# A retention and mixture-of-experts kernel: the second-to-last expert's chain two stages a step, and weight places given out earlier

## The chip, the cores and the metric

The kernel runs on one core of a Trainium2 chip. The metric is device time in microseconds of one execution; a run's time is compared with that of other runs of the same kernel. Engines: PE (TensorE, matmuls), DVE (VectorE), ACT (ScalarE), POOL (GpSimd) and SP, which here only issues DMAs. Each engine works through its own list of instructions in order and waits on semaphores.

## The reference

Three parts follow each other, all in float32:

```python
for t in range(S):                       # retention, 4 x 8 heads, S = 768, D = 64
    state = gamma * state + outer(k[t], v[t])
    y[t] = scale * q[t] @ state
# x: 3072 rows x 512.  Top-1 mixture, E = 8 experts, F = 1024
e = argmax(x @ w_gate)
out[i] = gate[i] * sigmoid(x @ w_output_gate)[i, e] * (relu(x[i] @ w1[e]) @ w2[e])
# soft mixture, 32 slots = 8 experts x 4
logits = out @ phi
slot_input = softmax(logits, over rows).T @ out
slot_out = relu(slot_input @ m_w1[e]) @ m_w2[e]
result = softmax(logits, over slots) @ slot_out
```

## The kernel before

Some 327 us are not touched by the change (retention, the gates, the lists of rows of each expert, and the stages of the first seven experts); only the stages of the last expert, and what follows, are.

The top-1 mixture goes expert by expert (`e`, 0 to 7, in an order set at run time), and each expert in KF = 8 stages `f`; `g = 8e + f` counts them. Stage `g` is `l1(g)` (L916 to L929): 12 matmuls of 128x128 by the expert's rows (L924: four k-tiles, each as w1-high by x-high, w1-high by x-low, w1-low by x-high), into one of two PSUM tiles, and one `relu` on ACT that leaves `h`. What the stage needs: the row of w1 (`load_w`, L214, three tiles `r`, issued three stages ahead), and its splitting into high and low (`split_w`, ACT `wh` L222 and DVE `wl` L223, two stages ahead). A `load_w` can go out when the `split_w` of the row three earlier is through.

The output of an expert isn't formed row by row. Instead each expert has a chain that makes logits of its rows and adds its share to the 32 slots:

- `logits` (PE L954, in two halves, `lps`), from `h` and a product of w2 and phi; `logit_parts` (ACT `ls` L961, DVE `ll` L962); `logit_sum` (PE L975 twice, then DVE `msk` L977 and three small ones, L979 to L981).
- `p_exp` (ACT L985, L986), `p_tr` (DVE `pd` L991 and two small ones).
- `slot_h` (PE L1037, 96 small matmuls, from `hB`, the turned `h`, and `pd`), `slot_s` (four copies `gr`, two on DVE and two on ACT, L1044), `slot_t` (PE `gsum` L1050, DVE `gt` L1053), `slot_in` (PE `slo` L1059, with the eight `w` pieces of w2), `slot_acc` (DVE `acc` L1063).
- beside it `c_tr` (DVE L1000), `c_exp` (DVE and ACT, L1004 to L1007) and `c_put` (DVE L1013 to L1017, then scatters `ctok` from POOL, L1020); `mask` (POOL L967) is made for the next expert.

This chain runs one expert late: `behind(e - 1, f)` (L1068) is called in stage `f` of expert `e`, behind `l1(g)`, and gives the chain's next part:

```python
if f == 0: logits(e, 1); slot_in(e - 1) if e; h_tr(e, 6); h_tr(e, 7)
f == 1: logit_sum    f == 2: p_exp     f == 3: p_tr     f == 4: slot_h, c_tr
f == 5: slot_s, c_exp     f == 6: slot_t, c_put
if 2 < f < 7: load_w2(e, (2 * f - 6, 2 * f - 5))
```

(here `e` is the expert ahead). Its `slot_in` falls into stage 0 of the expert after the next, its `slot_acc` and the next `logit_parts` into stage 1 (L1118 to L1122). For expert 6 there is no such stage: its `slot_in` and `slot_acc` stand behind the loop (L1183, L1184), between `logit_parts` and `logit_sum` of expert 7. The chain of expert 7 runs there alone, from L1181 to L1217, and its result `siT` starts the last part.

The last part (from L1225) is the soft mixture on the 32 slots. `f_l1` (L1234) and `f_l2` (L1268) read the second mixture's weights, 128 pieces `m` of 128x512 (256 KB each), in the order in which they were loaded; `emit_out` writes the result, 12 outputs of 256 KB for each half of the columns. 92 of the pieces are loaded before `f_l1` starts, into whatever tiles are free by then (`load_m2`, L269): own tiles `m2p`, then tiles of the w1 rows (`wraw`, `whl`), of the rows x (`xtp`, `xp`), of w2 (`w2p`, eight tiles, `wup`), and of `h` (`hp`, `hbp`). The other 36 go into tiles freed by the last part (`refill`).

All those loads are issued by SP, in program order: `load_w`, `load_w2` (L945) and `load_m2`. A load whose tile is still read waits, and all behind it wait too.

For expert 7 the first four `w` pieces go into the tiles `xp` (the gathered rows, "row places", free from stage 0 on) in stage 2 (L1167), the last four into `whl` in stages 6 and 7 (L1171). The eight `w2p` tiles get pieces `m` behind the loop (L1192), the `xp` tiles at the very end (L1219).

Of the kernel before, what the change touches and what calls it, by code (L numbers as in the profile page):

```python
# [22 lines left out]
E = 8  # L23
# [114 lines left out]
def retention_moe_kernel(ctx, tc, qt, kt, kn, vn, gates, moe_w1, moe_w2,  # L138
# [57 lines left out]
    def load_er(k):  # L196
        if k < E:
            er.append(nc.values_load(ordi[0:1, k:k + 1], engines=[mybir.EngineType.SP], min_val=0, max_val=E - 1))
# [77 lines left out]
    def load_m2(pool, tag, w=1):  # L276
        w = min(w, NM2 - len(m2_t))
        if w > 0:
            m2_into(pool.tile([128, w * 512], F32, tag=tag, name="m2"), w, (pool, tag, w) if w < 3 else None)
# [601 lines left out]
    with ExitStack() as pb:  # L881
# [49 lines left out]
        def h_tr(e, f):  # L931

            c = C[e]
            if f == 0:
                hB[e] = hbp.tile([128, NBX, KF, 32], F32, tag="hB", name="hB")
            nc.vector.transpose(out=hB[e][:, 0:NB[e], f, :], in_=hs[e * KF + f][:, 0:c].rearrange("p (b t) -> p b t", t=32))  # L936
# [5 lines left out]
        def load_w2(e, fs, pool=w2p, tag="w2"):  # L942
            for f in fs:
                w2n[e, f] = pool.tile([128, DM], F32, tag=tag, name="w2")
                nc.sync.dma_start(out=w2n[e, f], in_=moe_w2[0, bass.ds(er[e], 1), :, f * DM:(f + 1) * DM].rearrange("o p d -> (o p) d"))  # L945

        def logits(e, hf):

            c = C[e]
            if hf == 0:  # L950
                lps[e] = ps_1.tile([128, c], F32, tag="l", name="lps")
            for i in range(4):
                f = hf * 4 + i
                nc.tensor.matmul(out=lps[e][32 * i:32 * i + 32, :], lhsT=wp[e][:, f, :], rhs=hs[e * KF + f][:, 0:c],  # L954
                                 start=(hf == 0), stop=(hf == 1), skip_group_check=True)

        def logit_parts(e):
            c = C[e]
            hi, lo = lrs[e] = [sp.tile([128, CX], F32R, tag=n, name=n) for n in ("ls", "ll")]
            ps = lps.pop(e)  # L960
            nc.scalar.activation(out=hi[:, 0:c], in_=ps, func=ACTF.Copy)  # L961
            nc.vector.tensor_tensor(out=lo[:, 0:c], in0=ps, in1=hi[:, 0:c], op=ALU.subtract)  # L962
# [7 lines left out]
        def logit_sum(e):  # L970

            c = C[e]
            ps = lrs2[e] = ps_1.tile([128, 512], F32, tag="r", name="lsum")
            for n, part in enumerate(lrs.pop(e)):
                nc.tensor.matmul(out=ps[:, 0:c], lhsT=same_r, rhs=part[:, 0:c], start=(n == 0), stop=(n == 1))  # L975
            lm = lms[e] = msks.pop(e)
            nc.vector.tensor_tensor(out=lm[:, 0:c], in0=ps[:, 0:c], in1=lm[:, 0:c], op=ALU.add)  # L977
            sm = sms[e] = sp.tile([128, 8], F32, tag="smb", name="smb", bufs=2)
            nc.vector.tensor_reduce(out=sm[:, 0:1], in_=lm[:, 0:c], axis=AX.X, op=ALU.max)  # L979
            nc.vector.tensor_tensor(out=sm[:, 1:2], in0=sm[:, 0:1], in1=mrun, op=ALU.max)  # L980
            nc.vector.tensor_scalar(out=sm[:, 2:3], in0=sm[:, 1:2], scalar1=-1.0, scalar2=None, op0=ALU.mult)  # L981

        def p_exp(e):
            c, sm, lm = C[e], sms[e], lms[e]
            nc.scalar.activation(out=lm[:, 0:c], in_=lm[:, 0:c], func=ACTF.Exp, bias=sm[:, 2:3], accum_out=sm[:, 3:4])  # L985
            nc.scalar.activation(out=sm[:, 4:5], in_=mrun, func=ACTF.Exp, bias=sm[:, 2:3])  # L986
# [54 lines left out]
        def slot_s(e):  # L1041
            grs[e] = sp.tile([128, 4, 256], F32, tag="gr", name="gr")
            for a in range(4):
                (nc.scalar.copy if a % 2 else nc.vector.tensor_copy)(out=grs[e][:, a, :], in_=gps[e][a])  # L1044
# [10 lines left out]
        def slot_in(e):  # L1055
            ps = slo[e] = ps_1.tile([128, DM], F32, tag="C", name="slo")
            for f in range(KF):
                i = f % 4
                nc.tensor.matmul(out=ps[32 * i:32 * i + 32, :], lhsT=gts[e][:, f, :], rhs=w2n.pop((e, f)),  # L1059
                                 start=(f < 4), stop=(f >= 4), skip_group_check=True)  # L1060

        def slot_acc(e):
            nc.vector.scalar_tensor_tensor(out=acc, in0=acc, scalar=sms.pop(e)[:, 4:5], in1=slo.pop(e), op0=ALU.mult, op1=ALU.add)  # L1063

        def behind(e, f):

            if not 0 <= e < E:
                return  # L1068
            if f == 0:
                logits(e, 1)  # L1070
                if e:
                    slot_in(e - 1)
                h_tr(e, 6)
                h_tr(e, 7)
            elif f == 1:
                logit_sum(e)
            elif f == 2:
                p_exp(e)
            elif f == 3:
                p_tr(e)  # L1080
            elif f == 4:
                slot_h(e)
                c_tr(e)
            elif f == 5:
                slot_s(e)
                c_exp(e)
            elif f == 6:
                slot_t(e)
                c_put(e)
            if 2 < f < 7:  # L1090
                load_w2(e, (2 * f - 6, 2 * f - 5))

        load_er(1)

        after(load_w(1), gets[0])
# [12 lines left out]
        for g in range(G):  # L1108
            e, f = divmod(g, KF)
            if f == 0:  # L1110
                load_er(e + 2)
            if e + 1 < E and f < len(XT[e + 1]):

                gather(e + 1, (f,))
                if f:
                    after(gets[e + 1][f], [relu[-1]])
            split_w(g + 2)
            if e and f == 1:  # L1118

                if e > 1:  # L1120
                    slot_acc(e - 2)
                logit_parts(e - 1)  # L1122
            if g < G - 3:
                load_w(g + 3)
            else:
                load_m2(wraw, "r1")
            if g > 3 and g % 2 and len(m2_t) < NPRE:
                load_m2(m2p, "m2", 2)
            if f in (4, 5) and e + 1 < E:
                for j in range(2 * f - 8, min(2 * f - 6, len(XT[e + 1]))):  # L1130
                    x_scale(e + 1, j)
            if f == KF - 1 and e + 1 < E:

                xps = x_mm(e + 1, "ABDr", sorted(((j, kk) for kk in range(KD) for j in range(len(XT[e + 1]))),
                                                 key=lambda b: XT[e + 1][b[0]] < 128))
                l1(g, lambda: [x_split(e + 1, ps) for ps in xps])
            else:
                l1(g)
            behind(e - 1, f)


            if g == UMM:
                wq_mm(0, ps_1, "C")
                wq_add(0)
            if f == (1 if e else UMM):
                wq_turn(e, sp.tile([128, KF, NS], F32, tag="wp", name="wp"))
            if e + 1 < E:
                if f == (2 if e else 3):
                    part_load(e + 1)
                if e == 0 and f in (3, 4):  # L1150
                    for q in ((1, 2), (3,))[f - 3]:
                        wq_load(1, q, 1, wup, "wu")
                if f == (3 if e else 6):

                    wq_mm(e + 1, ps_1, "A" if e else "C")
                    wq_add(e + 1)
            if g == KF - 1:
                wq_load(2, 1, 1, wup, "wu")
                wq_load(2, 2, 1, wup, "wu")
            if g == KF:  # L1160
                wq_load(2, 3, 1, wup, "wu")
            if e and e + 2 < E and 4 <= f < 7:
                wq_load(e + 2, f - 3, 1, wup, "wu")
            elif G - 13 < g < G - 9:
                load_m2(wup, "wu", 2)
            if g == G - 6:
                load_w2(e, range(4), xp, "xy")  # L1167
            if g >= G - 2:

                for i, tag in enumerate(("wh1", "wl1")):  # L1170
                    load_w2(e, (2 * f - 8 + i,), whl, tag)  # L1171
            if f == 4:
                logits(e, 0)
            if f == 5:

                mask(e)
            if f >= 5:
                h_tr(e, 2 * f - 10)
                h_tr(e, 2 * f - 9)
        e = E - 1  # L1180
        logits(e, 1)  # L1181
        logit_parts(e)
        slot_in(e - 1)  # L1183
        slot_acc(e - 1)  # L1184
        logit_sum(e)
        load_m2(whl, "wh1")
        load_m2(whl, "wl1")
        for _ in range(KD):
            load_m2(xtp, "xh")
            load_m2(xtp, "xl")  # L1190
        for _ in range(8):
            load_m2(w2p, "w2")  # L1192
        h_tr(e, 6)
        h_tr(e, 7)
        for _ in range(NH):
# [20 lines left out]
        c_exp(e)  # L1216
        c_put(e)  # L1217
        for _ in range(4):
            load_m2(xp, "xy")  # L1219
        for _ in range(2):  # L1220
            load_m2(whl, "wh1")
            load_m2(whl, "wl1")
# [162 lines left out]
```

## Time and profile before

| | us |
|---|---|
| median of 3 runs | 430.12 (428.57 to 433.73) |
| the profiled execution | 429.54 |
| its span in the trace | 427.7 |

All times in the rows are of the profiled execution, counted from the span's start. The last expert's stages 0 to 7 start on PE at about 329.4, 334.2, 336.9, 339.0, 341.1, 346.0, 348.1 and 350.9 us; its own chain runs from 353.2 to 372.4, and the last part from there to the end. A fp32 matmul leaves two records (`x16` for the eight of `slot_in`).

### The profile page before, as it was taken

The page shows a single profiled execution, that of the slowest core. Times are in us where ns is not written, and L with a number is a line of the kernel's source. Part 1 is how long each engine was busy: PE and PEld are TensorE (multiplying, and loading weights), DVE is VectorE, ACT ScalarE, POOL GpSimd, SP SyncE. Part 2 cuts the span into 40 slices and gives each one's busy share as a digit, 9 for nine tenths or more (in the row PEclk, how much of TensorE's full clock was granted, in tenths as well). Part 3 has the DMA queues.
Part 4 walks back from the last instruction along what each step waited for, and adds up shares of the span by engine and source line. Part 5 has one row for each costly group of instructions (what it writes and reads, how often), then busy time and mean ns, then how long its engine had stood idle before and what let it go on. Part 6 is the DMA issues. An engine that isn't in the chain of part 4 may idle for free.

```text
span 427.7 us, 11525 instructions
## 1 busy us (share of the span) xinstructions
PE 378.0 (88%) x4398; PEld 283.7 (66%) x4398; DVE 260.6 (61%) x684; ACT 164.6 (38%) x368; POOL 107.7 (25%) x116
## 2 busy tenths in 40 slices
PE   2989999999537999999999999999999997799990
PEld 2867777776336768778877877687779873225560
DVE  1598989898632276485684765856767655414250
ACT  1532222233232365445545545534455421112332
POOL 2313333331121214043152331520622122020020
PEclk9999999999959989999999999999999997699996
DMA  7999999999667988986969959959778789999998
GB/s 268 400 422 357 276 322 344 351 327 270 162 198 269 304 304 278 393 301 219 405 223 316 390 186 364 355 191 393 261 239 320 241 268 310 391 391 408 395 336 288
DMA packets 67858, 132.96 MB, mean 311 GB/s; under 512 B 10612, under 2 KB 30066, under 8 KB 65362
## 3 DMA queue, kind: packets, MB, share of 16 engines
q1 hardware_dynamic: 61010, 120.17, 79.7%
q0 software_dynamic: 3344, 8.34, 6.4%
q10 hardware_dynamic: 3440, 3.63, 2.6%
q8 instruction: 36, 0.59, 0.6%
q14 instruction: 28, 0.23, 0.2%
HBM read 117.89 MB, written 14.25 MB: 309 GB/s over the span
## 4 chain that ended last, share of the span: by engine, by line
PE 64%; DMA 20%; DVE 6%; ACT 4%; issue 2%; SPq 1%; ACTq 1%; POOL 0%; DVEq 0%
PE hps L924 25%; DMA r<-in_moe_w_dram 7%; PE s L447 4%; DMA w<-in_moe_w_dram 4%; PE o L480 4%; DMA raw<-in_qt_dram 4%; PE fh L1238 4%; PE slo L1059 4%; PE so L1275 3%; PE gps L1037 3%; PE o L471 2%; PE lps L954 2%; DMA xg<-xs,xidx 2%; PE wps L243 2%; DMA wt<-in_moe_w_dram 2%; PE xps L902 2%
## 5 line engine op out<-in xcount | busy, mean ns | idle before, releaser
L924 PE MATMUL hps<-xh,wh 128*128 128x416 f32 (+2 forms) x256 | 92.1, 360 | 2.7 <-ACT h L929 2.6
L924 PE MATMUL hps<-xl,wh 128*128 128x416 f32 (+2 forms) x256 | 89.1, 348 | 1.2 <-DVE xl L912 1.1
L924 PE MATMUL hps<-xh,wl 128*128 128x416 f32 (+2 forms) x256 | 88.7, 346 | 0.0
L223 DVE TENSOR_TENSOR wl<-r,wh 128x512 fp32r<-128x512 f32 x64 | 43.3, 678 | 60.6 <-ACT wh L222 60.5
L222 ACT ACTIVATE wh<-r 128x512 fp32r<-128x512 f32 x64 | 40.2, 630 | 56.5 <-DMA r<-in_moe_w_dram 46.8
L924 PEld LDWEIGHTS hps<-xh,wh 128*128 128x128 f32 x256 | 48.0, 188 | 18.6 <-issue 13.9
L929 ACT ACTIVATE h<-hps 128x416 f32<-128x416 f32 (+2 forms) x64 | 32.6, 510 | 65.2 <-PE hps L924 65.2
L1020 POOL DMA_INDIRECT ctok<-ce,xidx x29 | 29.6, 1021 | 101.2 <-DVE ce L1017 94.8
L924 PEld LDWEIGHTS hps<-xl,wh 128*128 128x128 f32 x256 | 48.1, 188 | 2.9 <-DVE xl L912 2.3
L746 POOL DMA_INDIRECT xg<-xs,xidx x29 | 30.3, 1046 | 74.1 <-ACT h L929 41.9
L924 PEld LDWEIGHTS hps<-xh,wl 128*128 128x128 f32 x256 | 48.1, 188 | 0.7
L457 DVE TENSOR_TENSOR sS<-s,csa 128x512 f32<-128x512 f32 x48 | 30.4, 675 | 14.6 <-PE s L447 14.6
L447 PE MATMUL s<-raw 64*128 64x128 f32 x384 | 31.4, 298 | 8.3 <-DMA raw<-in_qt_dram 8.1
L936 DVE STREAM_TRANSPOSE hB<-h 128x416 f32<-128x416 f32 (+2 forms) x64 | 34.4, 576 | 0.0
L447 PEld LDWEIGHTS s<-raw 64*128 64x128 f32 x384 | 26.3, 198 | 10.9 <-DMA raw<-in_qt_dram 5.6
L480 PE MATMUL o<-sS,raw 128*64 128x128 f32 x384 | 27.1, 285 | 0.0
L429 POOL TENSOR_TENSOR k<-raw,cs 128x512 f32<-128x512 f32 x20 | 22.1, 1121 | 15.6 <-DMA raw<-in_qt_dram 13.2
L512 ACT COPY xT<-o 128x512 f32<-128x512 f32 x24 | 13.9, 580 | 31.3 <-PE o L480 31.3
L902 PE MATMUL xps<-cs,xg 128*128 128x128 f32 (+2 forms) x116 | 16.5, 298 | 9.1 <-DVE xg L893 9.1
L480 PEld LDWEIGHTS o<-sS,raw 128*64 128x64 f32 x384 | 21.2, 140 | 3.7 <-issue 3.4
L1037 PE MATMUL gps<-hB,pd 32*32 32x256 f32 x816 | 20.6, 413 | 3.1 <-DVE pd L991 3.1
L902 PEld LDWEIGHTS xps<-cs,xg 128*128 128x128 f32 (+2 forms) x116 | 14.2, 158 | 13.4 <-ACT wh L222 9.2
(175 smaller groups left out, 531.6 us busy)
## 6 DMA issues: line engine op xcount, KB each, us to landing
m<-in_moe_w_dram SPq DMA_DIRECT2D x41, 512.0 KB, 7.3
wt<-in_moe_w_dram SPq DMA_DIRECT2D x32, 512.0 KB, 7.1
r<-in_moe_w_dram SPq DMA_DIRECT2D x64, 256.0 KB, 4.4
w<-in_moe_w_dram SPq DMA_DIRECT2D x64, 256.0 KB, 6.0
m<-in_moe_w_dram SPq DMA_DIRECT2D x36, 256.0 KB, 5.9
xs<-xr SPq DMA_DIRECT2D x32, 192.0 KB, 8.4
raw<-in_kt_dram SPq DMA_DIRECT2D x5, 1024.0 KB, 10.2
raw<-in_kn_dram SPq DMA_DIRECT2D x5, 1024.0 KB, 6.8
```

What stands on the lines that cost most here:

```text
L222: nc.scalar.activation(out=hi, in_=t, func=ACTF.Copy)
L223: nc.vector.tensor_tensor(out=lo, in0=t, in1=hi, op=ALU.subtract)
L447: nc.tensor.matmul(out=ps[h][:, p, :], lhsT=kq(i, p, 0)[r], rhs=kq(i, p, 1)[r], start=True, stop=True, tile_position=(64 * h, 0), skip_gro ...
L457: nc.vector.tensor_tensor(out=sS[i][:, h], in0=sps.pop((i, h)), in1=con("dm", 128)[:, 4 * h:4 * h + 4, :], op=ALU.mult)
L480: nc.tensor.matmul(out=o_at(i, p, h), lhsT=vals(i, 2 * p + h), rhs=s[:, h, p, :], start=(i % NCH == 0 and n < 4), stop=True, skip_group_ch ...
L746: gets.setdefault(e, []).append(nc.gpsimd.indirect_dma_start(out=t[0:r, :], out_offset=None, in_=xs[:, :], in_offset=bass.IndirectOffsetOn ...
L902: nc.tensor.transpose(out=ps[kk][:, j * 128:j * 128 + r], in_=xg[e][j][0:r, kk * 128:(kk + 1) * 128], identity=ident[0:r, 0:r])
L924: nc.tensor.matmul(out=ps, lhsT=a[:, kk * 128:(kk + 1) * 128], rhs=x[e][kk][:, 0:c], start=(n == 0), stop=(n == 11))
L929: relu.append(nc.scalar.activation(out=hs[g][:, 0:c], in_=ps, func=ACTF.Relu))
L936: nc.vector.transpose(out=hB[e][:, 0:NB[e], f, :], in_=hs[e * KF + f][:, 0:c].rearrange("p (b t) -> p b t", t=32))
L1020: put = nc.gpsimd.indirect_dma_start(out=ctok[:, :], out_offset=bass.IndirectOffsetOnAxis(ap=xidx[0:r, e, j:j + 1], axis=0), in_=cn[0:r, j ...
L1037: nc.tensor.matmul(out=ps[a][32 * j:32 * j + 32, :], lhsT=pd[q, b, :], rhs=hB[e][q, b].rearrange("p f t -> p (f t)"), start=(i == 0), stop ...
```

## The change

A second function, `behind_last`, takes the place of `behind` while the last expert's stages run. In it the chain of expert 6 has two parts in most steps, so that `slot_in` and `slot_acc` fall into stages 5 and 6, and are gone behind the loop. `logit_parts` of expert 6 comes in stage 0 instead of stage 1. The eight `w` pieces of expert 6 are loaded in stages 0 to 3. The four tiles `xp` take pieces `m` in stages 0 to 3; the first four `w` pieces of expert 7 go into `w2p` in stage 5, behind `slot_in` of expert 6, and four pieces `m` into the other `w2p` tiles; the other four `w2p` places are filled at the end, where the `xp` places were. The diff:

```diff
...
             if 2 < f < 7:
                 load_w2(e, (2 * f - 6, 2 * f - 5))
 
+        def behind_last(e, f):
+
+            if f == 0:
+                logits(e, 1)
+                slot_in(e - 1)
+                logit_parts(e)
+                h_tr(e, 6)
+                h_tr(e, 7)
+            elif f == 1:
+                logit_sum(e)
+            elif f == 2:
+                p_exp(e)
+                p_tr(e)
+            elif f == 3:
+                slot_h(e)
+                c_tr(e)
+            elif f == 4:
+                slot_s(e)
+                slot_t(e)
+                c_exp(e)
+            elif f == 5:
+                slot_in(e)
+                c_put(e)
+            elif f == 6:
+                slot_acc(e)
+            if f < 4:
+                load_w2(e, (2 * f, 2 * f + 1))
+            elif f == 5:
+                load_w2(e + 1, range(4))
+                for _ in range(4):
+                    load_m2(w2p, "w2")
+
         load_er(1)
 
         after(load_w(1), gets[0])
...
 
                 if e > 1:
                     slot_acc(e - 2)
-                logit_parts(e - 1)
+                if e < E - 1:
+                    logit_parts(e - 1)
             if g < G - 3:
                 load_w(g + 3)
             else:
...
                 l1(g, lambda: [x_split(e + 1, ps) for ps in xps])
             else:
                 l1(g)
-            behind(e - 1, f)
+            (behind if e < E - 1 else behind_last)(e - 1, f)
 
 
             if g == UMM:
...
                 wq_load(e + 2, f - 3, 1, wup, "wu")
             elif G - 13 < g < G - 9:
                 load_m2(wup, "wu", 2)
-            if g == G - 6:
-                load_w2(e, range(4), xp, "xy")
+            if G - KF <= g < G - KF + 4:
+                load_m2(xp, "xy")
             if g >= G - 2:
 
                 for i, tag in enumerate(("wh1", "wl1")):
...
         e = E - 1
         logits(e, 1)
         logit_parts(e)
-        slot_in(e - 1)
-        slot_acc(e - 1)
         logit_sum(e)
         load_m2(whl, "wh1")
         load_m2(whl, "wl1")
         for _ in range(KD):
             load_m2(xtp, "xh")
             load_m2(xtp, "xl")
-        for _ in range(8):
-            load_m2(w2p, "w2")
         h_tr(e, 6)
         h_tr(e, 7)
         for _ in range(NH):
...
         c_exp(e)
         c_put(e)
         for _ in range(4):
-            load_m2(xp, "xy")
+            load_m2(w2p, "w2")
         for _ in range(2):
             load_m2(whl, "wh1")
             load_m2(whl, "wl1")
```

## Rows read from the trace of the kernel before

**Rows 1.** The page's chain that ended last, by engine (share of the span).
```profile
PE 64%; DMA 20%; DVE 6%; ACT 4%; issue 2%; SPq 1%; ACTq 1%; POOL 0%; DVEq 0%
```

**Rows 2.** Stretches: length, busy PE, PEld, DVE, ACT, POOL; clock, DMA share, GB/s.
```profile
326.00:334.00 8.00, 8.00 (x64) 6.04 (x60) 7.68 (x18) 4.91 (x11) 4.47 (x4) 1.00 0.53 177
342.00:350.00 8.00, 8.00 (x134) 6.37 (x133) 4.75 (x15) 2.47 (x7) 2.08 (x1) 1.00 0.82 278
358.00:369.00 11.00, 7.56 (x120) 2.59 (x120) 3.32 (x11) 1.54 (x5) 0.00 (x0) 0.54 1.02 373
378.00:412.00 34.00, 33.30 (x415) 16.72 (x408) 10.55 (x40) 8.88 (x20) 1.55 (x2) 1.00 1.04 396
413.40:427.70 14.30, 3.65 (x24) 3.04 (x24) 4.46 (x7) 4.00 (x7) 0.86 (x2) 0.74 0.90 295
```

**Rows 3.** The chain in order of time, 343 to 378 us: start, length, what.
```profile
343.15 2.06 PE gps L1037 x88
...
350.94 2.31 PE hps L924 x12
...
354.35 0.23 PE slo L1059 x3
354.57 0.10 PE lps L954
354.67 1.73 PE slo L1059 x13
...
357.09 0.56 DVE msk L977
...
360.08 3.46 PE gps L1037 x96
```

**Rows 4.** The chain in order of time, 326 to 345 us.
```profile
331.73 0.78 PE lps L954 x8
332.51 1.72 PE slo L1059 x16
...
336.88 6.27 PE hps L924 x36
```

**Rows 5.** Single instructions in order of time, of PE, ACT and DVE, 347 to 365 us.
```profile
347.96 0.33 PE L924 MATMUL hps<-xh,wl 128*128 128x384 f32 x1
...
348.33 0.49 ACT L929 ACTIVATE h<-hps 128x384 f32<-128x384 f32 x1 [3.98 <-PE hps L924]
348.71 0.65 ACT L1044 COPY gr<-gps 128x256 f32<-128x256 f32 x2
...
355.23 0.56 DVE L962 TENSOR_TENSOR ll<-lps,ls 128x384 fp32r<-128x384 f32 x1 [0.99 <-ACT ls L961]
...
356.60 0.33 PE L975 MATMUL lsum<-ll,same_r 128*128 128x384 f32 x1
...
364.32 1.08 PE L1050 MATMUL gsum<-gr,cs 128*32 128x256 f32 x8 [0.79 <-DVE gr L1044]
```

**Rows 6.** Single instructions of ACT, DVE and POOL, 339 to 345 us.
```profile
339.41 0.61 ACT L985 ACTIVATE msk<-msk,smb 128x384 f32<-128x384 f32 x1
...
341.45 0.57 DVE L991 STREAM_TRANSPOSE pd<-msk 128x384 f32<-128x384 f32 x1
...
342.20 2.08 POOL L967 TENSOR_SCALAR msk<-cs,rt 128x384 f32<-128x384 f32 x1 [9.04 <-DVE srun L993]
```

**Rows 7.** SP's issue of one w1 row; landing times of L214, 325 to 345 us.
```profile
329.04 0.33 SPq L214 DMA_DIRECT2D r<-in_moe_w_dram  x1
...
DMA to landing us min/median/max: 2.7/4.3/5.2
```

**Rows 8.** The tile `two`, 380 us to the end: durations ns min/median/max, first and last start.
```profile
L1275 PE MATMUL so<-two x40: 379/379/403, 408.2 to 411.0; 128*32 128x256 f32 x40
...
L269 SPq DMA_DIRECT2D two<-in_moe_w_dram x10: 328/382/1196, 395.1 to 403.7; - x10
...
DMA to landing us min/median/max: 4.8/6.3/7.9
```

## The prediction

> **What bounds the kernel now.** I read the page's chain first: PE has 64% of it and DMA 20% [rows 1], so PE mostly decides. Then the stretches around the change: from 326 to 350 us, where the last expert's stages run, PE is busy without a gap at full clock (1.00, 2.4 GHz), while the DMA engines are busy 0.53 to 0.82 at 177 to 278 GB/s; from 378 to 412 us both are full (PE 33.3 of 34 us, DMA share 1.04 at 396 GB/s) [rows 2]. So inside the loop each microsecond given to PE is a microsecond of time, and DMA has room; behind it DMA has none. Third, the chain in order of time from 343 us on [rows 3]: the last stage, `lps`, `slo` of the expert ahead, then a DVE series that starts with `msk`, then PE again, one after the other.
>
> **In the loop, what is added to PE.** Write e for the last expert, e-1 for the one ahead. Three terms.
>
> (1) `slot_in(e-1)` moves from behind the loop to stage 5. The same 16 records (for e-2) took 1.72 us in stage 0 of this expert [rows 4]; PE has no idle time there to hide them: +1.72.
>
> (2) `slot_s` and `slot_t` now stand in one stage, with no stage between them. `slot_t` needs the copies `gr`; two of the four are on ACT, and there the `relu` of that stage is ahead of them, which cannot start before the stage's last matmul. The trace shows this distance for a stage: the last matmul ends at 347.96 + 0.33 = 348.29, the `relu` (`h`) starts at 348.33, the ACT copies end at 348.71 + 0.65 = 349.36 [rows 5]. In the old order a stage of PE work covered it; now PE stands still over the distance and a hand-over of 0.04: +1.11. What is queued behind on PE is `logits(e, 0)` and all later stages. That PE waits for every copy is seen behind the loop, where `gsum` stood idle 0.79 us until DVE's were done, with nothing ahead of the copies [rows 5]. Bounds: 0.33, if the 0.78 us of `lps` [rows 4] got past the waiting matmuls, and 1.90, the distance and that idle time one after the other. I take 1.11, the row of the same situation.
>
> (3) When PE returns to a stage after other work its 12 matmuls take 2.31 us [rows 3] instead of 6.27 / 3 = 2.09 [rows 4]. From stage 2 on there were two such returns, now there are three: +0.22.
>
> Sum in the loop: +3.05.
>
> On (2) the Trainium skill, "TensorE: Matmul & The Clock Gate", section "Part 3: Packing small matmuls — row/col tiling", says that matmuls start and end strictly in program order and only weight loads are pulled ahead; by that the stop is the full 1.11. This trace has three `slo` of the next group ahead of the last `lps` [rows 3], which does not look like it; if such passing helped here the sum would be 0.78 lower. I keep the distance, because a stop on a semaphore holds what is behind it in all the rows of [rows 5].
>
> **Edits that I cost at nothing, with their cover.** `p_tr(e-1)` goes one stage ahead: on DVE it waits for the exponential, which ACT ran at 339.41 for 0.61 us; `pd`, 0.57 us, then ends near 340.8 [rows 6]. Stage 3 ends on PE at 336.88 + 2 x 2.09 = 341.06 [rows 4], where `slot_h` now starts: 0.3 us of cover, and each microsecond beyond is PE time. `logit_parts`, `c_tr`, `c_exp` and `slot_acc` lie on ACT and DVE, busy 2.5 and 4.8 of the 8 us from 342 on [rows 2]. `c_put(e-1)` now goes ahead of `mask(e)` on POOL, which takes 2.08 us and had ended by 344.3 [rows 6]; it is needed only at the last `lsum`, 356.6 before. It would have to come 12 us later to cost anything; it now comes behind the scatters of stage 5, some ten microseconds later, so of this cover little may be left, and beyond it each microsecond would delay `msk`. The DMAs: eight `w` pieces of e-1 move from stages 3 to 6 to stages 0 to 3, four `w` pieces of e from stage 2 to stage 5, and eight pieces `m` come ahead of the end of the loop. The bytes are the same; what their order does is the rivals'.
>
> **Behind the loop.** `slo` (1.73 us) and `acc` leave. But PE was not the last to be ready there: `lps` ends at 354.67, ACT then takes `ls`, DVE `ll` until 355.23 + 0.56 = 355.79, and the second `lsum`, 0.33 us, could end at 356.16 [rows 3, 5]. So `msk` starts at about 356.20 instead of 357.09: -0.89. Of the 1.73 us only half was on the path; the other half lay under `ls` and `ll`. Bounds: -0.16, if `lsum` ended only as it did (356.60 + 0.33) and `acc` alone goes, and -1.73. What follows, from `msk` to the end of the chain of e, stays as it is. There PE ran at 1.2 GHz for most of the time (clock 0.54 from 358 to 369 us [rows 2]), after it had nothing to do from 356.93 to 360.08; `slot_h` takes 3.46 us there and 2.06 at full clock [rows 3]. Its idle time ahead of `slot_h` hardly changes, so I change nothing; a drop at another place is worth 1.4 us either way.
>
> Net on the chain: +3.05 - 0.89 = +2.16.
>
> **The end.** From 413.4 us to the end DMA moves 14.3 us x 295 GB/s = 4.22 MB [rows 2]; by the order of the last part, 14 of the 24 outputs of 256 KB, 3.67 MB, are made after that. So 0.55 MB were left over from before, 1.4 us at 396 GB/s; where PE is later and the loads are not, part of it has gone by then. Between 0 and -1.4 I take half, -0.7. Sum: +2.16 - 0.7, about +1.5. The profiled execution took 429.54 us (span 427.7), so 431.0. The median of the runs before is 430.12 (428.57 to 433.73); from there the same sum gives 431.6.
>
> **Rival one: the weight stream sets the end, faster.** The last ten pieces are issued from 395.1 to 403.7 and take 6.3 us to land, so the last one lands at about 410.0; PE's last matmul on them starts at 411.0 [rows 8]. That is 1 us from deciding. The change lets pieces out ahead of the loop's end, where DMA has room [rows 2]. If four more of them, 1.05 MB, have landed by 358 us, the stream ends 1.05 / 0.39 = 2.7 us sooner, and if the end follows the stream: 429.54 - 2.7 = 426.8. Against it: PE is idle only 0.7 of 34 us from 378 on, so PE gives the end, not the stream. And SP issues in order and now stands ahead of `load_w2(e)` from about 342 us until `slot_in(e-1)` near 350, so what is gained in stages 0 to 3 is lost there.
>
> **Rival two: the w1 rows come late, slower.** In stage 0 SP now waits for the first matmuls of `slot_in(e-2)`, at about 333 us (332.51 and a little [rows 4]), before it issues the next row `r` of w1, which went out at 329.04 before [rows 7]. Behind two `w` and one `m` it goes out near 334.2. With the 4.3 us of these loads (2.7 to 5.2 [rows 7]) it lands at 338.5, and the copy `wh`, which stands ahead of the `relu` and the exponential on ACT, is just in time. With the 7.9 us of a full DMA [rows 8] it lands at 342.1; `wh`, `relu`, the exponential and `pd` follow in about 2.3 us (0.65, 0.4, 0.7 and 0.55 by the starts in [rows 5, 6]), to 344.4, and `slot_h`, which wants `pd` at 341.1, stops PE 3.3 us: 431.0 + 3.3 = 434.3. It decides from a landing at about 338.7 on. For it: fifteen pieces want to go out in ten microseconds, the rate of a full DMA. Against it: this row is among the first four, while DMA is still empty.
>
> **How the numbers follow.** Forecast (429.8 to 433.0) 0.52; rival one 0.20; rival two 0.20; a clock drop at another place, 1.4 us on either side, 0.08. The range that leaves out at most 2 in 10 takes in both rivals, 426.8 and 434.3, and about 1 us for where a median lies (that of before is 0.6 from its profiled execution): 425.8 to 435.4. A measurement of this kernel tells about 2%, 8.6 us, from no change. No case reaches that: faster 0.02, same 0.95, slower 0.03.
>
> **What would show it.** Right: from the start of stage 2 to the last matmul of stage 7 about 3 us more; one idle time on PE of about 1.1 us ahead of `gsum` in stage 4, put down to `gr`; `slo` of e-1 in stage 5 with 1.7 us; `msk` of e about 1.5 us after the last `lps`; `m` issues standing still from about 342 to 350. Wrong: no idle time before that `gsum`; PE waiting for `pd` or `wl` in stages 3 to 5 (rival two); the weights landing well ahead of the last matmuls and the end earlier (rival one); `msk` waiting for POOL's mask.

## The result, and the profile after

| | before | changed |
|---|---|---|
| median of 15 runs, us | 429.85 (428.08 to 433.73) | 434.15 (431.33 to 436.40) |
| ratio, 95% interval | | 1.0102 (1.0081 to 1.0123) |
| profiled execution, us (span) | 429.54 (427.7) | 435.06 (433.3) |

The changed kernel is 1.0% slower, 4.3 us: the same within 2%, but clear of the noise. The forecast was 431.0 (429.8 to 433.0 for the forecast case by itself, 425.8 to 435.4 for the whole range). The time lies in the range and outside the forecast case: it is nearly what rival two gave, 434.3.

To see where it came from, both traces are cut at four places: the end of the last expert's `xps` (its rows turned, ahead of the last stage of expert 6), the end of the last L924 matmul, the first `msk` behind that, and the first matmul of the last part (`fh`).

| us | before | changed | difference | forecast |
|---|---|---|---|---|
| stages (`xps` end to last L924: the last one of expert 6, then 0 to 7) | 25.73 | 32.28 | +6.55 | +3.05 |
| to `msk` | 3.83 | 3.14 | -0.69 | -0.89 |
| `msk` to `fh` | 15.32 | 14.18 | -1.14 | 0 |
| last part, `fh` to the end of the span | 55.29 | 56.69 | +1.40 | -0.7 |
| sum | 100.17 | 106.29 | +6.12 | +1.5 |

In this pair of executions the sum is 6.1 us; the stages ahead of it were 0.5 us shorter in the changed kernel's. The medians differ by less, 4.3.

The stages, from the chain in order of time of the changed kernel:

```profile
331.99 1.72 PE slo L1059 x16
...
336.37 2.12 PE hps L924 x12
...
340.00 5.69 DMA r<-in_moe_w_dram
...
345.77 0.64 ACT wh L222
...
346.43 0.69 DVE wl L223
...
347.15 0.43 DVE gr L1044
...
347.73 0.65 PE gsum L1050 x5
...
349.52 3.56 PE hps L924 x12
353.07 1.85 PE slo L1059 x16
354.93 4.37 PE hps L924 x24
359.29 1.43 PE lps L954 x8
```

Before, this chain was PE alone [rows 3, 4]. Now it leaves PE at 338.5 and goes over a load of a w1 row `r`, issued at 340.00 and landed at 345.69, the copies `wh` and `wl` made of it, and `gr`, to `gsum`. Where PE itself stood, in its own rows of the changed kernel (in brackets the idle time ahead and what ended it):

```profile
341.26 2.12 PE L1037 MATMUL gps<-hB,pd 32*32 32x256 f32 x96 [0.71 <-DVE pd L991]
...
347.73 0.65 PE L1050 MATMUL gsum<-gr,cs 128*32 128x256 f32 x6 [2.05 <-DVE gr L1044]
348.15 0.52 PE L954 MATMUL lps<-h,wp 128*32 128x384 f32 x2
348.20 0.39 PE L1050 MATMUL gsum<-gr,cs 128*32 128x256 f32 x2
```

The 6.55 us are: `slo` 1.85; the two stops 0.71 + 2.05 = 2.76; the stage behind the second stop 3.56 instead of 2.31 us, and `gsum` and `lps` ahead of that stage 1.79 (347.73 to 349.52) instead of 0.57 + 0.78, together 1.69; one more return, 0.22 by the forecast. That is 6.52.

Most of the stage of 3.56 us ran at 1.2 GHz: the granted clock is 0.50 from 348.7 to 352.2 us and 1.00 on either side. The stretches of the changed kernel (columns as in [rows 2]):

```profile
326.00:334.00 8.00, 8.00 (x60) 5.88 (x59) 6.98 (x18) 5.01 (x10) 4.47 (x4) 1.00 0.33 117
342.00:350.00 8.00, 5.95 (x94) 3.96 (x93) 4.08 (x11) 2.94 (x8) 0.00 (x0) 0.93 0.75 275
350.00:358.00 8.00, 8.00 (x46) 6.31 (x45) 5.09 (x12) 1.43 (x3) 4.52 (x4) 0.86 0.36 96
358.00:369.00 11.00, 6.62 (x114) 3.28 (x112) 4.12 (x12) 2.35 (x7) 0.00 (x0) 0.86 1.00 362
378.00:412.00 34.00, 32.00 (x367) 14.46 (x360) 9.83 (x39) 6.68 (x16) 2.99 (x3) 0.98 1.01 388
```

The stretch from 350 to 358 us of the kernel before:

```profile
350.00:358.00 8.00, 6.93 (x49) 3.69 (x47) 5.22 (x13) 1.47 (x3) 2.98 (x3) 1.00 0.83 258
```

Two things are to be seen. The mean clock is 0.93 and 0.86 from 342 to 358, where it had been 1.00: it fell after PE had stood 0.71 and 2.05 us, about 1 us after PE had gone on. And DMA moves 117 instead of 177 GB/s from 326 to 334 us, and 96 GB/s from 350 to 358, where it moved 258 before. The last of those has its reason in SP's list (start, time over which the issues of the line go, line, issues):

```profile
325.44 0.33 SPq L214 DMA_DIRECT2D r<-in_moe_w_dram  x1
332.86 0.91 SPq L945 DMA_DIRECT2D w<-in_moe_w_dram  x2
333.96 0.34 SPq L269 DMA_DIRECT2D m<-in_moe_w_dram  x1
334.88 0.34 SPq L214 DMA_DIRECT2D r<-in_moe_w_dram  x1
...
337.77 0.33 SPq L214 DMA_DIRECT2D r<-in_moe_w_dram  x1
...
340.00 0.33 SPq L214 DMA_DIRECT2D r<-in_moe_w_dram  x1
...
342.91 0.33 SPq L214 DMA_DIRECT2D r<-in_moe_w_dram  x1
344.26 0.34 SPq L269 DMA_DIRECT2D m<-in_moe_w_dram  x1
354.08 2.12 SPq L945 DMA_DIRECT2D w<-in_moe_w_dram  x4
```

From 344.6 to 354.1 SP issues nothing, since it stands ahead of the `w` pieces that wait for `slot_in`. The w1 row that had gone out at 329.04 [rows 7] goes out at 334.88, behind two `w` and one `m`; the three rows after it at 337.77, 340.00 and 342.91 (332.42, 335.99 and 339.47 before). The stream of weights is later too: the tile `two` of the changed kernel, as in [rows 8]:

```profile
L1304 PE MATMUL so<-two x40: 379/379/403, 413.8 to 416.6; 128*32 128x256 f32 x40
...
L269 SPq DMA_DIRECT2D two<-in_moe_w_dram x10: 328/355/999, 401.9 to 410.8; - x10
```

The last weight goes out at 410.8 instead of 403.7, 7.1 us later, while PE came to the last part 4.2 us later (376.61 instead of 372.41). Between that issue and the last matmul on such a piece there are 5.8 us now, 7.3 before. But PE doesn't wait for a last weight there. Where the last part lost its time, the chain shows:

```profile
386.79 5.88 DMA m<-in_moe_w_dram
392.69 7.31 DMA two<-ctok
...
400.80 1.12 PE ctps L1329 x12
```

The second read of the scattered rows goes out on ACT's queue when a load `m` has landed, and takes 7.31 us; PE stands 0.34 us ahead of `ft` and 1.16 us ahead of `ctps`, which is most of the 1.40.

### The profile page after: what moved, and what is told of

Read it like the earlier page. It is cut to its first block, busy times and chain, and to the rows that moved or that the text cites. A ratio compares the mean times of both kernels' runs of the same rounds, so it can differ in the third digit from the quotient of the medians.

```text
span 433.3 us, 11524 instructions
## 1 busy us (share of the span) xinstructions
PE 379.4 (88%) x4398; PEld 284.3 (66%) x4398; DVE 260.6 (60%) x684; ACT 165.5 (38%) x368; POOL 108.3 (25%) x116
## 3 DMA queue, kind: packets, MB, share of 16 engines
q10 hardware_dynamic: 3440, 3.63, 2.5%
## 4 chain that ended last, share of the span: by engine, by line
PE 68%; DMA 13%; DVE 7%; ACT 4%; issue 3%; SPq 2%; ACTq 1%; another core or an unknown queue 0%; POOL 0%; DVEq 0%
PE hps L924 28%; PE s L447 5%; PE o L480 4%; PE gps L1037 4%; DMA raw<-in_qt_dram 4%; PE slo L1059 4%; DMA r<-in_moe_w_dram 3%; PE lps L954 3%; PE xps L902 3%; PE so L1304 3%; PE o L471 3%; PE fh L1267 2%; DMA xg<-xs,xidx 2%; PE wps L243 2%; DMA two<-ctok 2%
## 5 line engine op out<-in xcount | busy, mean ns | idle before, releaser
L924 PE MATMUL hps<-xh,wh 128*128 128x416 f32 (+2 forms) x256 | 93.2, 364 | 1.5 <-ACT h L929 1.4
L924 PE MATMUL hps<-xl,wh 128*128 128x416 f32 (+2 forms) x256 | 90.0, 352 | 0.4 <-issue 0.4
L924 PE MATMUL hps<-xh,wl 128*128 128x416 f32 (+2 forms) x256 | 89.4, 349 | 0.0
L924 PEld LDWEIGHTS hps<-xh,wh 128*128 128x128 f32 x256 | 48.7, 190 | 18.3 <-issue 14.6
L924 PEld LDWEIGHTS hps<-xl,wh 128*128 128x128 f32 x256 | 48.8, 190 | 2.1 <-DVE xl L912 0.7
L924 PEld LDWEIGHTS hps<-xh,wl 128*128 128x128 f32 x256 | 48.8, 191 | 0.7
L902 PE MATMUL xps<-cs,xg 128*128 128x128 f32 (+2 forms) x116 | 15.3, 284 | 9.1 <-ACT wh L222 9.1
L902 PEld LDWEIGHTS xps<-cs,xg 128*128 128x128 f32 (+2 forms) x116 | 13.0, 149 | 12.9 <-ACT wh L222 9.2
```

The lines of the kernel that those rows point to most:

```text
L902: nc.tensor.transpose(out=ps[kk][:, j * 128:j * 128 + r], in_=xg[e][j][0:r, kk * 128:(kk + 1) * 128], identity=ident[0:r, 0:r])
L924: nc.tensor.matmul(out=ps, lhsT=a[:, kk * 128:(kk + 1) * 128], rhs=x[e][kk][:, 0:c], start=(n == 0), stop=(n == 11))
```

## The experiments

All are timed in five rounds beside the kernel before. Each profile is one execution; the table cuts it as above, and "sum" is from the end of `xps` to the end of the span.

| run | ratio to before (95%) | stages | to `msk` | to `fh` | last part | sum |
|---|---|---|---|---|---|---|
| before | | 25.73 | 3.83 | 15.32 | 55.29 | 100.17 |
| changed | 1.0102 (1.0081 to 1.0123) | 32.28 | 3.14 | 14.18 | 56.69 | 106.29 |
| slot_t a stage later | 1.0076 (1.0048 to 1.0104) | 29.76 | 3.58 | 15.05 | 55.30 | 103.69 |
| w1 rows first | 1.0043 (1.0016 to 1.0070) | 29.04 | 3.13 | 14.72 | 56.18 | 103.07 |
| both | 1.0079 (1.0047 to 1.0112) | 28.00 | 3.13 | 15.11 | 55.28 | 101.52 |
| both, again | 1.0061 (1.0032 to 1.0089) | 28.04 | 3.14 | 14.96 | 55.80 | 101.94 |
| places back | 1.0132 (1.0100 to 1.0164) | 32.22 | 3.13 | 13.13 | 57.44 | 105.92 |
| slot_in alone | 1.0043 (1.0009 to 1.0076) | 26.62 | 5.38 | 14.71 | 55.05 | 101.76 |
| slot_t joined alone | 1.0031 (1.0004 to 1.0058) | 26.92 | 3.83 | 14.21 | 55.92 | 100.88 |
| w pieces early alone | 1.0050 (1.0019 to 1.0080) | 27.47 | 4.49 | 15.39 | 55.26 | 102.61 |
| sum ahead of slot_in | 0.9987 (0.9961 to 1.0013) | 25.73 | 3.13 | 12.16 | 57.28 | 98.30 |
| the same, again | 0.9973 (0.9949 to 0.9998) | 25.78 | 3.13 | 12.15 | 58.26 | 99.32 |
| the same, scatters early | 0.9984 (0.9947 to 1.0021) | 27.23 | 3.13 | 12.53 | 58.13 | 101.02 |
| changed, scatters early | 1.0097 (1.0061 to 1.0133) | 31.28 | 3.14 | 15.91 | 55.90 | 106.23 |

One execution can be longer where nothing of an edit is: "slot_in alone" and "the same, scatters early" have 0.9 and 1.5 us more in the stages than their edits reach, in part in waits inside their first two stages. The part ahead of the cut, which no edit touches, ends at 327.0 to 330.3 us in these fourteen profiles. So a difference of 1 to 2 us between two rows is no proof by itself; the single stops named below, and the ratios, are what the argument rests on.

**`slot_t` one stage later**, in the changed kernel:

```diff
                 slot_s(e)
-                slot_t(e)
                 c_exp(e)
             elif f == 5:
-                slot_in(e)
+                slot_t(e)
                 c_put(e)
             elif f == 6:
+                slot_in(e)
+            elif f == 7:
                 slot_acc(e)
...
-            elif f == 5:
+            elif f == 6:
                 load_w2(e + 1, range(4))
```

> The changed kernel with slot_t one stage behind slot_s again (slot_t and c_put in stage 5, slot_in and the four first w pieces of the last expert in stage 6, slot_acc in stage 7). Theory A (the loop: PE stopped 2.1 us ahead of gsum and ran the next stage at 1.2 GHz, 3.56 us instead of 2.31): the stop goes and with it the slow stage, 2 to 3.4 us less than the changed kernel, ratio to before about 1.003. Theory B (the stream: SP stands ahead of the w pieces until slot_in, DMA at 96 GB/s from 350 to 358 us): SP stands one stage longer, so the time is the changed kernel's or up to 1.5 us more, ratio 1.010 to 1.014. Theory C (slot_in's own 1.7 us of PE time is what costs): no change, ratio 1.010.

The stop ahead of `gsum` is gone, and no stage runs at the half clock; the stages take 2.5 us less than the changed kernel's. PE still waits for `pd`, here 1.14 us. The stops go as A had it, but A's 1.003 lies outside the interval of 1.0076: the sum of this profile, 103.69, is still 3.5 us above that of before, 1.85 of it `slo` and 1.14 the wait for `pd`. B's extra cost in the last part didn't come (55.30).

**The w1 rows first**, in the changed kernel:

```diff
-            if f < 4:
-                load_w2(e, (2 * f, 2 * f + 1))
+            if 0 < f < 5:
+                load_w2(e, (2 * f - 2, 2 * f - 1))
```

> The changed kernel with the eight w pieces of the expert ahead loaded in stages 1 to 4 instead of 0 to 3, so that the w1 row for stage 4 is issued at about 329 us again, ahead of the wait for slot_in. Theory A, with late rows as the cause of the longer stop (wh waited for its row until 345.77 and held relu and the copies back): the row copies come 2 to 4 us earlier, PE's wait for pd (0.7) goes, that for gr shrinks from 2.1 to 1.1 us, and the clock may not drop: 1.5 to 3 us less, ratio 1.003 to 1.007. Theory B: SP stands at the same place, no change, 1.010. Theory C: no change, 1.010.

In the loop all is as A has it. In this run's rows of single instructions:

```profile
346.50 0.49 ACT L929 ACTIVATE h<-hps 128x384 f32<-128x384 f32 x1 [2.04 <-PE hps L924]
346.88 0.64 ACT L1044 COPY gr<-gps 128x256 f32<-128x256 f32 x2
...
347.58 0.64 PE L1050 MATMUL gsum<-gr,cs 128*32 128x256 f32 x8 [1.12 <-ACT gr L1044]
```

PE waits 1.12 us for the two copies on ACT that stand behind the `relu`, and not at all for `pd`; the clock is 1.00 up to the end of the stages. The stages take 29.04 us, 3.31 more than before, where the forecast had 3.05. So 3.2 us of the changed kernel's stages were the late rows and what they brought; by the times the edit is worth 2.5 us (1.0102 less 1.0043).

**Both edits together:**

> The changed kernel with both edits of the two runs before: slot_t one stage behind slot_s, and the w pieces of the expert ahead in stages 1 to 4, so that the w1 rows go out first. Theory A (late rows and the joined stages are what stops PE): no stop at pd or gsum, no slow stage; left is slot_in's 1.85 us and 0.2 for one more return, less 0.7 behind the loop: +1.4 us to before, ratio 1.003, under both single edits. Theory D (any order with slot_in inside the loop costs as much, since the time moves to the next late thing): ratio as the better single edit, 1.004 or more.

> The changed kernel with slot_t a stage later and the w pieces in stages 1 to 4, once more: by the trace of the first run +1.35 us in the part that is touched, ratio 1.003; by its times 1.0079 (1.0047 to 1.0112). If the trace is right, about 1.003 to 1.005; if a cost lies in front of the last expert that one profile does not show, 1.008 again.

By the trace A holds twice: no stop, no slow stage, 28.0 us of stages, a sum of +1.35 and +1.8. By the times it does not: 1.0079 and 1.0061 are +3.4 and +2.6 us, no less than the single edit of the rows, and that is what theory D had. In both profiles the rest stands ahead of the cut: `xps` ends at 329.68 and 330.26 us, 2.2 and 2.7 us later than before, with the same code up to there. Three other runs end it as late (330.1 to 330.2), so it can be chance; two out of two may be more. The cause stays open, and with it whether A or D is right.

**The places as before**, with the changed chain: `load_w2(e, range(4), xp, "xy")` in stage 2 again, no `m` in `xp` or `w2p` inside the loop, eight behind it.

```diff
-            elif f == 5:
-                load_w2(e + 1, range(4))
-                for _ in range(4):
-                    load_m2(w2p, "w2")
...
-            if G - KF <= g < G - KF + 4:
-                load_m2(xp, "xy")
+            if g == G - 6:
+                load_w2(e, range(4), xp, "xy")
```

> The changed kernel with the places as before: the last expert's first four w pieces in the row places in stage 2, no pieces m there and in the w2 places inside the loop, eight pieces m in the w2 places behind it; the chain keeps its two parts a step. Theory B: SP no longer stands from 344 to 354 us, the stream is again well ahead and the end, 1.4 us of which came in the last part (scatters' rows read back late, ctps waiting), comes 1.4 to 3 us sooner, ratio 1.003 to 1.007. Theory A: the loop is as in the changed kernel or a little worse, since four more w pieces go out ahead of the late rows: 1.010 to 1.013. Theory C: 1.010.

No better than the changed kernel, as A had it at its upper end, and B falls in this form: the last part takes 57.4 us, and SP stands here too, from 348.4 to 353.8, ahead of `w` pieces whose tiles a stage (L924) still reads. DMA moves 111 GB/s from 350 to 358 us, 96 in the changed kernel. So giving the places out early was not what cost; here SP found another tile that wasn't free.

**`slot_in` and `slot_acc` alone in the loop** (stage 7), in the kernel before:

```diff
+            elif f == 7 and e == E - 2:
+                slot_in(e)
+                slot_acc(e)
...
         logit_parts(e)
-        slot_in(e - 1)
-        slot_acc(e - 1)
         logit_sum(e)
```

> The kernel before with only slot_in and slot_acc of the expert ahead put into stage 7 of the loop; all else stays where it was, places and loads too. Theory C: the 1.7 us come in full, less 0.9 behind the loop and up to 0.4 for the relu that they now cover: +0.4 to +0.8 us, if C is the main cost +3 or more, ratio 1.007. Theories A and B: little, ratio 1.001 to 1.002.

```profile
356.76 1.85 PE slo L1059 x16
```

From the last stage to `msk` it takes 1.55 us more: the 1.85 us of `slot_in` stand there in full, ahead of `lps`, and what it had covered (PE waits 1.75 us for `ls`) is idle time. 0.6 came back up to `fh`. So by this profile moving `slot_in` costs about 1 us net, more than the 0.4 to 0.8 expected, and is not the main cost. The times, +1.85 us (0.4 to 3.3), agree with that but don't exclude C's 1.007.

**`slot_t` joined to `slot_s` alone**, in the kernel before (`slot_t` of the expert ahead in stage 5 instead of 6, for the last expert only):

```diff
             elif f == 5:
                 slot_s(e)
+                if e == E - 2:
+                    slot_t(e)
                 c_exp(e)
```

> The kernel before with only slot_t of the expert ahead put into the stage of slot_s (stage 5); slot_in, loads and places stay. Theory A with rows on time: PE stops 1.1 us ahead of gsum, put down to the ACT copies behind relu, and nothing else: +1.1 us, ratio 1.0026; no drop of the clock inside the loop. If such a stop alone brought the half clock with it: +2.3 us, ratio 1.005.

```profile
349.21 0.64 PE L1050 MATMUL gsum<-gr,cs 128*32 128x256 f32 x8 [1.12 <-ACT gr L1044]
```

The stop is 1.12 us again, put down to ACT's `gr`, the stages take 1.19 more, and no stage runs slow. The ratio, 1.0031 (+0.2 to +2.5 us), fits the 1.1 to 1.2 us.

**The `w` pieces early alone**, in the kernel before:

```diff
-            if 2 < f < 7:
+            if e < E - 2 and 2 < f < 7:
                 load_w2(e, (2 * f - 6, 2 * f - 5))
+            elif e == E - 2 and f < 4:
+                load_w2(e, (2 * f, 2 * f + 1))
```

> The kernel before with only the eight w pieces of the expert ahead loaded in stages 0 to 3, ahead of the w1 rows that follow them; the chain and the places stay. If late rows cost only where the chain has no stage between its parts: the rows come 4 to 6 us later and wh with them, but nothing on PE waits: 0 to +0.5 us, ratio 1.000 to 1.001. If the late rows stop PE by themselves (rival two of the prediction): +1 to +3 us, PE waiting for wl or pd in stages 3 to 6, ratio 1.003 to 1.007.

Late rows stop PE by themselves, even with the chain as before. The chain in order of time of this run:

```profile
337.60 5.34 DMA r<-in_moe_w_dram
...
343.03 0.64 ACT wh L222
...
343.70 0.69 DVE wl L223
...
344.39 0.50 DVE pd L991
...
344.93 2.12 PE gps L1037 x88
```

`pd` stands behind `wl` on DVE, `wl` needs `wh`, and `wh` the row; PE stands 0.83 us for it. The stages take 1.7 us more in this profile, 0.5 of it in the first two, ahead of the edit, and `msk` comes 0.7 us later behind the last stage. The ratio is 1.005, +2.1 us (0.8 to 3.4): by the times this edit alone makes about half of the changed kernel's loss.

**`logit_sum` ahead of `slot_in` behind the loop**, in the kernel before:

```diff
         logits(e, 1)
+        h_tr(e, 6)
+        h_tr(e, 7)
         logit_parts(e)
+        logit_sum(e)
         slot_in(e - 1)
         slot_acc(e - 1)
-        logit_sum(e)
...
-        h_tr(e, 6)
-        h_tr(e, 7)
```

> The kernel before, all stages as they were, with another order behind the loop only: the last two turns of h ahead of logit_parts, then logit_sum, and slot_in and slot_acc of the expert ahead behind it. If half of slot_in's time was on the path there (my step): msk starts 0.9 us sooner after the loop, slot_in lies under the DVE series, and slot_h starts 0.9 us sooner; PE is idle for only some 1.2 instead of 3.1 us ahead of slot_h, so the clock may also stay at full for it, 1.4 us more: -0.9 to -2.3 us, ratio 0.995 to 0.998. If slot_in was no part of the path: 1.000.

> The kernel before with logit_sum ahead of slot_in behind the loop, once more, beside the one above: by the trace of the first run 1.9 us less in the part that it touches, ratio 0.9955; by its times 0.9987 (0.9961 to 1.0013). The two agree near 0.996 to 0.997.

Up to `fh` it does more than expected, 3.9 us in both profiles. `slot_in` lies under the DVE series, PE's idle time ahead of `slot_h` is 1.44 us instead of 3.15, and the clock stays up. The chain in order of time of the first of the two, and its stretch:

```profile
358.85 1.98 PE slo L1059 x16
...
362.15 2.13 PE gps L1037 x87
...
366.27 2.04 PE slo L1059 x16
```

```profile
358.00:369.00 11.00, 7.25 (x138) 2.50 (x138) 5.05 (x13) 1.54 (x5) 0.82 (x1) 1.00 1.01 349
```

`gps` takes 2.13 us instead of 3.46 [rows 3], the clock is 1.00 instead of 0.54 [rows 2]. But the last part takes 2.0 and 3.0 us longer. The chain of the first profile, and a row of PE, show where:

```profile
382.28 5.90 DMA m<-in_moe_w_dram
388.20 6.48 DMA two<-ctok
...
395.49 1.12 PE ctps L1300 x12
```

```profile
389.29 1.14 PE L1259 MATMUL ft<-cs,two 128*128 128x128 f32 x8 [1.09 <-ACT two L1242]
```

ACT issues the read of the scattered rows (`two<-ctok`) ahead of a `relu` (`two`, L1242), and by the profile the read waits for a load `m`. So PE stood 1.09 us for the `relu` and 0.50 us ahead of `ctps` for the rows; before it was 0.21 and nothing. In the second profile PE stood 3.00 us for that `relu`. The stream of weights is near its limit besides. The tile `two` of the first of these runs:

```profile
L1275 PE MATMUL so<-two x40: 379/379/403, 408.5 to 411.5; 128*32 128x256 f32 x40
...
L269 SPq DMA_DIRECT2D two<-in_moe_w_dram x10: 327/328/495, 397.4 to 406.0; - x10
```

Its last weight goes out 75.9 us after the end of its `xps` (330.10), before 76.2 after it (403.7 - 327.53): the stream did not move. PE's last matmul follows 5.5 us after that issue, where there were 7.3. In the fourteen profiles this distance is 5.4 to 7.9 us, and in two of them ("w1 rows first" and "places back", 5.8 and 6.1) PE waits 0.4 and 0.7 us for a last weight. So without the stops PE could not have come much sooner either. How much each of the two holds isn't shown. The sums fell by 1.9 and 0.9 us; the times say 0.9987 and 0.9973, the first with 1 in its interval, so about 0.9 us is what can be claimed.

**The scatters early**, on that version and on the changed kernel:

```diff
         load_m2(hbp, "hB", 7)
+        c_tr(e)
+        c_exp(e)
         slot_s(e)
         slot_t(e)
+        c_put(e)
         slot_in(e)
...
-        c_tr(e)
-        c_exp(e)
-        c_put(e)
```

> The order behind the loop of the earlier run (logit_sum ahead of slot_in of the expert ahead) together with the early scatters of the last expert, on the kernel before. That run was 3.9 us faster up to the last part and gave 2.0 back in it. If it gave them back to the late read of the scattered rows (ctps waits 0.5, ft 1.1): last part 55.5 to 56, 3 to 4 us faster than before, ratio 0.991 to 0.994. If to the weight stream, which ends where it did: last part 57, ratio 0.996 to 0.998.

> The changed kernel with c_tr, c_exp and c_put of the last expert pulled ahead of its slot_s and slot_in (into DVE's idle time during slot_h), so that its scatters go out some 8 us sooner. In the changed kernel ACT waited for them before it could read the rows back (issued 14.9 us after the last part's start, 12.3 before), and the last part took 56.7 us instead of 55.3. If that is the 1.4 us: the last part goes back to 55.3 or less, no waiting of ctps for c, 1.2 to 1.6 us less than the changed kernel, ratio to before about 1.007. If the late weights alone make it: last part 56.5, PE waiting for a weight instead, ratio 1.010.

On the first it brought nothing: last part 58.13 us, ratio 0.9984. The scatters started 3.7 us ahead of the last part instead of 1.9 us behind its start, but ACT issued the read of the scattered rows at 387.86 all the same (386.99 and 384.45 in the two profiles without this edit), waiting for a load `m` by the profile, and PE stood 3.2 us for the `relu` behind it. So it wasn't the scatters that held the read. Why the read waits for that load isn't shown. On the changed kernel the read goes out no sooner either, at 392.68 instead of 391.53. There `ctps` no longer waits and the last part is 0.8 us shorter, half of what was expected; but PE reached the last part 3.9 us later in that profile, which alone gives the read more time, and the time did not move, 1.0097. Its stages had stops of 1.46 and 1.80 us:

```profile
345.19 2.12 PE L1037 MATMUL gps<-hB,pd 32*32 32x256 f32 x96 [1.46 <-DVE pd L991]
```

```profile
352.92 2.31 PE hps L924 x12
```

## Why the prediction was right, and where it was not

The sign was right and the time is in the range, but not in the forecast case's own 429.8 to 433.0: it is rival two's mechanism, given 0.20, that came. The forecast's 1.5 us should be set beside the run with the w1 rows first: it is the change without rival two, and it came to 1.0043, +1.85 us (0.7 to 3.0; +2.9 in its profile). So the forecast case and rival two came together, where I had set one against the other. That the measured 434.15 is so near rival two's 434.3 is in part luck, as the sizes below show.

*Terms that held.* `slot_in` in the loop, 1.72: 1.85. The stop between `slot_s` and `slot_t`, 1.11: 1.12 in the two runs where rows are on time. The price of one more return, 0.22: what is left in the sum of the stages fits it, though no run measures it by itself. Behind the loop -0.89: -0.69; `lps` ends 1.43 us after the last stage as before (1.42), and the second `lsum` took 0.46 us instead of 0.33, having PE to itself. On the Trainium skill's rule of program order ("TensorE: Matmul & The Clock Gate", "Part 3: Packing small matmuls — row/col tiling"), the trace agrees on the stop: no `lps` got past the waiting `gsum` (347.73), the first record of one starts at 348.15, and the stop is the full distance. Among records whose wait is over, two of `lps` start ahead of the last two of `gsum` (348.15 and 348.20), as with `slo` and `lps` in [rows 3]; that saved none of the stop.

*The step that failed* is "Edits that I cost at nothing", in the part on the DMAs and on `pd`. I gave the late rows to a rival and let the first of them decide, at a landing of 338.7. It landed at about 338.9 (`wh` starts at 338.99), 0.2 later, in an execution whose stages stand 0.5 us earlier, and cost the 0.71 us ahead of `slot_h`. But four rows went out 3.4 to 5.8 us later than before, ACT's `wh` waited for three of them, and I had asked only about one. The third, 340.00 to 345.69, falls into the stage in which `slot_s` and `slot_t` stand together, and there `wh`, `relu` and the ACT copies of `gr` queue on ACT, `wl` and the DVE copies on DVE, all behind the row. That turned 1.11 into 2.05. Then, PE having stood twice, the clock fell for 3.5 us (a cost of 1.69), which I had looked for only behind the loop. Rival two's price of 3.3 was close to what came, 0.71 + 0.94 + 1.69 = 3.3, by luck: I had it as one stop at `pd`, and that stop was 0.71.

*The end* was wrong in sign: +1.40 for -0.7. I had the loads as not later, although I had written under rival one that SP would stand from about 342 to 350. SP's stop of 9.5 us and the empty stretch from 326 to 333 put the stream 7.1 us back, PE only 4.2, so the 7.3 us between the last issue and the last matmul shrank to 5.8, and the read of the scattered rows, behind a load `m`, came late (`ctps` stood 1.2 us). Rival one had it right that the stream is near to deciding (1 us by the landing; where PE waits for a last weight, in "w1 rows first" and "places back", the distance is 5.8 and 6.1, 1.2 to 1.5 less than before), with the sign the other way: the change moved the stream back, not ahead.

*What partly hid it:* from `msk` to `fh` 1.14 us were gained, which I had as nothing or 1.4 either way. The mean clock of this stretch is 0.74, and 0.67 before: `gps` took 3.03 us instead of 3.46, `slo` 2.94 instead of 3.63. PE had stood 3.10 us ahead of `gps`, 3.15 before, so why the clock came back sooner isn't shown. In the runs that leave this code as it is the stretch takes 13.1 to 15.4 us.

The mask, the other cover that I called thin, held: it ended at 357.6 and `msk` started at 362.43.

## What to carry to other kernels

When a load is pulled ahead in an in-order DMA list and its tile isn't free, ask for every load queued behind it, not only the next one, when it will land and which engine's list it then holds: a weight row that goes out three stages ahead has little cover left when it is 3.4 to 5.8 us late and a stage takes 2.1. Work that covers a wait of the path is not free to move: here it is worth more under the wait behind the loop, one place further on, than in a loop in which PE is full. And where a chain ends beside a full stream, see what waits for the stream before counting a gain: 3.9 us less on the chain gave about 1, since PE then stood for a read that waited behind a load, and the last weights were hardly 2 us ahead.

## What the runs showed of the hardware

I had not expected a drop of the clock inside the stages. In the changed kernel PE stood 0.71 and 2.05 us, with 4.4 us of work between the two; the granted clock was still 1.00 up to 348.7 and 0.50 (1.2 GHz) from there to 352.2, and the next stage took 3.56 instead of 2.31 us; in the run with the places back it was 0.54, 2.13, and 3.36 us. Single stops of 1.1 us ("w1 rows first", "`slot_t` a stage later", "`slot_t` joined alone") took nothing from the clock, and stops of 1.46 and 1.80 us in the last run didn't either (the stage behind them took 2.31). Those two make 3.26 us, more than the 2.76 and 2.67 us of the two cases in which the clock fell, so the sum of the stops doesn't tell the cases apart. Both drops had one stop of over 2 us; whether that is the reason wasn't tried, and these are three profiles.
